# Weight preparation spread over an attention stage, and side work of the following MLP moved between items

## The chip, the core and the metric

The kernel runs on one core of a Trainium2 chip. Its engines are TensorE (PE in the rows; its weight loads are PEld), VectorE (DVE), ScalarE (ACT) and GpSimd (POOL); all loads and stores are issued on SyncE's queue (SP). Each engine works through its own queue in order. The metric is the device time in microseconds.

## What is computed

Three models in a row, on 2304 tokens of 512 features. Inputs are fp32; the products run on fp16 halves of scaled operands.

```python
# 1: causal attention with decay, 4 batches x 8 heads, S = 576, D = 64
scores = q @ k.T / 8 + decay;  attn = softmax(causal(scores));  x = attn @ v      # -> (2304, 512)
# 2: MLP with cosine
h = x @ w_in;  x = (h * cos(h)) @ w_out                                            # 512 -> 2048 -> 512
# 3: MoE, 8 experts, gate normalised over rows and columns eight times
P = sinkhorn(exp(x @ w_gate - max));  out = sum_e P[:, e] * (relu(x @ w1[e]) @ w2[e])   # 512 -> 1024 -> 512
```

## The kernel before

The program's order is written out by hand and nothing is rescheduled: each engine executes its instructions as the code issues them.

**Stages.** The attention takes 0 to about 240 us. It goes through 16 pairs of heads, seven steps `x` a pair, 112 steps, and a few more in which the pipeline drains. The MLP takes 240 to 645 us. Its 2048 hidden features are 16 units of 128, in blocks `b` of 3, 4, 5 and 4 units; its tokens are five chunks `j` of 384, 384, 512, 512 and 512. An item is one unit on one chunk, 80 items in the order block, chunk, unit. For each item `layer1` issues 12 products into a bank, `between` computes h cos(h) with three operations of ScalarE (L283, L286, L289) and three of VectorE (L285, L288, L291), and two items later (`LAG`) `layer2` issues 12 products into the output tile. When the last unit of a block is through, `finish` takes the sum out (L970, L972, L974). The MoE fills the rest.

**Weight units.** The MLP's weights arrive as 64-bit words in fp32 pairs and are put into fp16 halves a unit at a time. `read_unit` takes two half units of 128x512: for each a guard product `dm` on GpSimd (L175), four operations on VectorE (L176, L178, L180, L183, the last of which reads `dm`) and a square on ScalarE (L185). `scale_unit` finds the scale. `split_unit` scales each half on ScalarE (L202) and splits it on GpSimd (L164, L165). A `yield` ends each piece. In the attention one piece is issued in every second step from step 4, and in every step from 104; units 0 to 2 are through by step 86, unit 3 is read in steps 88 to 104 and scaled in 105 to 107. The rest follows between the items, from `work`.

**Other side work.** `split_row` splits the attention's output on GpSimd (L227, L164, L165); the last chunk's rows are split at items 1, 3, 5 and 7. The survey takes the absolute maximum of the MoE's weights: 64 looks of 128x1024 on ScalarE (L906), each on a 512 KB load (L902) into one of two buffers, one look in each of items 0 to 63. `find_scale` makes a scale of the results: of w1 after item 32, of w2 after item 64, of x0 (the MoE's input of chunks 0 and 1) from item 70. `split_x` prepares a chunk for the gate with four times ScalarE L991 and VectorE L992 and L993; for chunks 0 and 1 all four at once, where the block is finished, at items 64 and 68. `scale_first` (L1087) scales x0 at items 73 and 74; GpSimd's `combine_first` (L1308, L1309, L1312) builds the MoE's operands of it.

Of the kernel before, what the change touches and what calls it, by code (L numbers as in the profile page):

```python
# [23 lines left out]
def kernel(  # L24
# [39 lines left out]
    TOP = 14  # L64
    LIMIT = 36
# [30 lines left out]
    dm = big.tile([P, DM], BF16, name="dm")  # L96
    XT = [big.tile([P, 2, KD, n], F16, name=f"xt{j}") for j, (_, n) in enumerate(CH)]
    spare_bank = []
    sq = big.tile([P, NQ * P], BF16, name="sq")
# [66 lines left out]

    def read_unit(u):
        tm, ws = tmw[u % len(tmw)], wsum[u % 3]
        for half in range(2):
            n = 2 * u + half  # L170
            words = stg[n % 2].rearrange("p (c two) -> p c two", two=2)
            top, low, topf = words.bitcast(I32)[:, :, 1], words.bitcast(I32)[:, :, 0], words[:, :, 1]
# [10 lines left out]
            nc.vector.scalar_tensor_tensor(x, dm, TINY * TINY, x, ALU.is_ge, ALU.mult)  # L183
            yield
            nc.scalar.activation(sq[:, 0:DM], x, AF.Square, accum_out=ws[:, half : half + 1])  # L185
# [62 lines left out]

    turns = {}
# [24 lines left out]
    def between(b, j, i, ps):  # L274
        n = CH[j][1]
        u = unit(b, i)
# [17 lines left out]
    with tc.manual_schedule():  # L294

        with ExitStack() as actx:
# [22 lines left out]
            E4 = ap1.tile([P, SP], F32, name="e4")  # L319
            v_hi = [ap1.tile([P, NF, 2, D + 1], F16, name=f"vh{i}") for i in range(2)]  # L320
# [151 lines left out]
            def square_v(n):  # L472
                vr = raw[n][2]
                nc.scalar.activation(
                    sq.rearrange("p (t h d) -> p t h d", h=2, d=D), vr[:, :, :, 0:D], AF.Square,
# [312 lines left out]
            pieces = chain(chain.from_iterable(run_unit(u) for u in range(NWA)), read_unit(NWA), scale_unit(NWA))  # L788
# [41 lines left out]
            for x in range(-9, NSTEP + PS):  # L830
# [13 lines left out]
                if x >= 4 and (x % 2 == 0 or x >= NSTEP - 8):  # L844
                    next(pieces, None)
# [4 lines left out]
                if x == NSTEP - 2 * PS:  # L850
# [3 lines left out]
                if x == NSTEP - 3:  # L854
                    assert not list(scaling)
# [4 lines left out]
            for _ in pieces:  # L860
# [862 lines left out]
```

## Time and profile before

| | us |
|---|---|
| median of 3 runs (1983.05 to 1984.57) | 1984.53 |
| the profiled execution | 1984.58 |
| its span | 1982.9 |
| busy: TensorE / VectorE / ScalarE / GpSimd | 1925.6 / 1481.5 / 1207.2 / 1112.9 |

TensorE is busy for 97% of the span, the granted clock of the span is 0.998 of full speed. A row of busy time by stretch gives for each engine the busy microseconds in it, with the instructions in brackets, then the granted clock, the busy share of the DMA engines and what they moved. In a timeline a row stands for one or several equal instructions in a row, with start, duration, engine, line, operation and tiles; in square brackets is how long the engine had been idle before it, and what ended that.

### The profile page before, as it was taken

Reading aid. Unit: us, or ns where it says so; the run is one execution under the profiler, and the core shown is the slowest. Engines: PE = TensorE matmul, PEld = TensorE weight load, DVE = VectorE, ACT = ScalarE, POOL = GpSimd, SP = SyncE. Lnnn points to the kernel's source line nnn. Section 1 sums busy time; section 2 is a strip of 40 time slices with the busy share of each in tenths; the row PEclk is TensorE's granted clock in tenths of the full one; section 3 lists DMA queues with packets and bytes.
Section 4 is the critical chain, followed back from the end, with each engine's and each line's share of the span. In section 5 each row is a group of like instructions: output and inputs, shape, how many; then the busy total and the mean of one; then the engine's idle time right before and its main releaser. Section 6 shows DMA issues by size and latency. Waiting matters only on the chain.

```text
span 1982.9 us, 38801 instructions
## 1 busy us (share of the span) xinstructions
PE 1925.6 (97%) x14490; PEld 1371.4 (69%) x14490; DVE 1481.5 (75%) x3263; ACT 1207.2 (61%) x2439; POOL 1112.9 (56%) x1549
## 2 busy tenths in 40 slices
PE   6999989999999999999999999999999999999998
PEld 5788745454544677777777777777777777777776
DVE  8888788786566578887777777777777777777776
ACT  7999778777644765555565555555555555556543
POOL 6788875323067886454654555645556555565531
PEclk9999999999999999999999999999999999999999
DMA  5545355553302022202022021220212202122022
GB/s 127 113 97 119 76 172 180 156 172 118 117 22 78 19 81 89 75 25 88 33 78 78 23 89 33 78 78 22 89 33 78 78 22 88 33 78 78 12 88 65
DMA packets 133916, 157.51 MB, mean 79 GB/s; under 512 B 63840, under 2 KB 98016, under 8 KB 133728
## 3 DMA queue, kind: packets, MB, share of 16 engines
q1 hardware_dynamic: 133728, 155.03, 25.9%
q8 instruction: 114, 1.87, 0.4%
q14 instruction: 74, 0.61, 0.1%
HBM read 139.71 MB, written 10.37 MB: 76 GB/s over the span
## 4 chain that ended last, share of the span: by engine, by line
PE 81%; DVE 9%; ACT 6%; POOL 2%; issue 2%; DVEq 0%; ACTq 0%; POOLq 0%
PE y L1588 19%; PE y L1467 18%; PE bq L1588 14%; PE bq L1467 14%; PE a L956 7%; PE ph L264 6%; DVE A L680 1%; ACT E L648 1%; ACT A L672 1%; DVE ph L288 1%; PE pst L660 1%; ACT t L286 1%; DVE acc L974 1%; DVE xl L992 1%; DVE t L285 1%
## 5 line engine op out<-in xcount | busy, mean ns | idle before, releaser
L1588 PEld LDWEIGHTS <-h 128*128 128x128 f16 x6048 | 590.6, 98 | 77.0 <-POOL h L1502 1.2
L1467 PEld LDWEIGHTS <-wa 128*128 128x128 f16 x4032 | 394.4, 98 | 259.2 <-issue 5.0
L1467 PE MATMUL y<-xc,wa 128*128 128x384 f16 x2304 | 430.6, 327 | 1.8 <-ACT ct L1483 1.0
L1502 POOL TENSOR_TENSOR h<-rt,h 128x384 f16<-128x384 f32 x192 | 175.5, 914 | 452.9 <-ACT h L1501 446.3
L1588 PE MATMUL y<-wb,h 128*128 128x256 f16 x3456 | 408.9, 273 | 0.9 <-POOL h L1502 0.9
L1483 ACT ACTIVATE ct<-y 128x384 f32<-128x384 f32 x192 | 94.4, 492 | 422.8 <-PE y L1467 422.6
L1467 PE MATMUL bq<-xc,wa 128*128 128x384 f16 x1728 | 329.1, 327 | 0.2 <-ACT ct L1483 0.2
L1588 PE MATMUL bq<-wb,h 128*128 128x256 f16 x2592 | 306.7, 273 | 0.2 <-DVE h L1493 0.2
L1569 DVE SCALAR_TENSOR_TENSOR acc<-y,gate,acc 128x256 f32<-128x256 f32 x504 | 212.6, 478 | 48.9 <-PE y L1588 48.9
L956 PE MATMUL a<-H,w 128*128 128x512 f16 (+1 forms) x960 | 201.4, 359 | 8.1 <-ACT acc L970 3.1
L264 PE MATMUL ph<-xt,w 128*128 128x512 f16 (+1 forms) x960 | 199.8, 358 | 0.0
L1569 DVE SCALAR_TENSOR_TENSOR acc<-bq,gate,acc 128x256 f32<-128x256 f32 x378 | 159.7, 478 | 39.2 <-PE bq L1588 39.1
L956 PEld LDWEIGHTS <-w 128*128 128x128 f16 x960 | 93.3, 98 | 102.7 <-issue 12.6
L1493 DVE TENSOR_TENSOR h<-bq,h 128x384 f16<-128x384 f32 x288 | 158.1, 551 | 3.3 <-ACT h L1490 0.6
L1487 DVE SCALAR_TENSOR_TENSOR bq<-bq,ct 128x384 f32<-128x384 f32 x192 | 107.7, 561 | 64.9 <-PE bq L1467 64.0
L264 PEld LDWEIGHTS <-w 128*128 128x128 f16 x960 | 93.5, 99 | 89.6
L1487 DVE SCALAR_TENSOR_TENSOR bq<-y,ct 128x384 f32<-128x384 f32 x96 | 54.4, 566 | 123.5 <-PE y L1467 118.1
L1490 ACT CAST h<-bq 128x384 f16<-128x384 f32 x288 | 134.7, 484 | 14.2 <-DVE bq L1544 14.0
L1496 POOL TENSOR_TENSOR h<-st,h 128x384 f16<-128x384 f32 x96 | 87.9, 916 | 84.9 <-ACT h L1490 79.8
L1500 ACT ACTIVATE rt<-bq 128x384 f32<-128x384 f32 x192 | 93.7, 488 | 21.5 <-DVE bq L1487 18.8
L1248 POOL TENSOR_TENSOR tm<-sg 128x256 f32<-128x256 f32 x128 | 92.4, 733 | 15.1 <-POOL h L1496 12.3
L1501 ACT ACTIVATE h<-bq 128x384 f16<-128x384 f32 x192 | 94.3, 491 | 0.0
(269 smaller groups left out, 3219.6 us busy)
## 6 DMA issues: line engine op xcount, KB each, us to landing
xc<-xd SPq DMA_DIRECT2D x105, 384.0 KB
seen<-in_moe_w_dram SPq DMA_DIRECT2D x64, 512.0 KB
sg<-in_moe_w_dram SPq DMA_DIRECT2D x64, 512.0 KB
stg<-in_moe_w_in_dram SPq DMA_DIRECT2D x16, 512.0 KB
stg<-in_moe_w_out_dram SPq DMA_DIRECT2D x16, 512.0 KB
xd<-xc SPq DMA_DIRECT2D x14, 384.0 KB
q<-q SPq DMA_DIRECT2D x30, 160.0 KB
out_dram<-acc SPq DMA_DIRECT2D x18, 256.0 KB
```

The lines of the kernel that those rows point to most:

```text
L264: nc.tensor.matmul(ps[:, 0:n], w[:, ws, kk * P : (kk + 1) * P], XT[j][:, xs, kk, :], start=first, stop=kk == KD - 1 and (ws, xs) == PASSES ...
L956: nc.tensor.matmul(a_of[b, j][x][:, 0:n], w[:, s1, DM + x * P : DM + (x + 1) * P], H[:, s2, 0:n], start=i == 0 and n_ == 0, stop=end and n ...
L1467: nc.tensor.matmul(ps[:, 0:HN], w[:, ws, a, k, :], X[b][:, xs, k, :], start=fresh and n == 0, stop=n == 5, skip_group_check=not fresh,)
L1483: nc.scalar.activation(c, cut(ps), AF.Copy, scale=RAISE)
L1487: nc.vector.scalar_tensor_tensor(cut(c), cut(ps), RAISE, other, ALU.mult, ALU.add)
L1490: nc.scalar.copy(HT[m][c][:, 0, :], src)
L1493: nc.vector.tensor_tensor(HT[m][c][:, 1, :], src, HT[m][c][:, 0, :], ALU.subtract)
L1500: nc.scalar.activation(r, cut(ps), AF.Relu)
L1501: nc.scalar.activation(HT[m][c][:, 0, :], cut(ps), AF.Relu)
L1502: nc.gpsimd.tensor_tensor(HT[m][c][:, 1, :], r, HT[m][c][:, 0, :], ALU.subtract)
L1569: nc.vector.scalar_tensor_tensor(a, v, gate[:, tt, e : e + 1], a, ALU.mult, ALU.add)
L1588: nc.tensor.matmul(ps[:, at_ * HD : (at_ + 1) * HD], HT[m][a][:, s1, c * P : (c + 1) * P], W2T[side][m][:, s2, b, :], start=fresh and m == ...
```

## The change

1. In the attention the pieces of units 0 to 2 come at 46 in 102 steps, evenly, from step 6 to 97. Unit 3 is read in the drain, one piece a step from step 107; its scaling moves behind the first items. The factors that depend on units 0 to 2 are formed at step 109 instead of 98 and 109.
2. In the attention GpSimd scales the unit's halves, in place of ScalarE; between the items ScalarE still does (`late_`).
3. The guard product is issued half a unit ahead, into one of two buffers.
4. No look in items 0 to 7, one in items 8 to 35, two in each from 36 until they are done (item 53). The scale of w1 and w2 follow then: w2's small operations move from items 65 to 68 to items 55 to 58.
5. Chunks 0 and 1 of the gate are split two rows at a time, behind the next two items' own operations.
6. x0's scale is found from item 71, `scale_first` runs at items 74 and 75, and the last chunk's rows are split at items 2, 4, 6 and 8.

The number of instructions on TensorE and VectorE stays.

```diff
+    dms = [big.tile([P, DM], BF16, name=f"dm{i}") for i in range(2)]
...
+    def guard(n):
+        if n < len(jobs):
+            top = words_of(n)[2]
+            nc.gpsimd.tensor_tensor(dms[n % 2], top, top, ALU.mult)
...
     def read_unit(u):
...
-            nc.gpsimd.tensor_tensor(dm, topf, topf, ALU.mult)
+            if n == 0:
+                guard(0)
             nc.vector.tensor_scalar(xi, top, 3, 0x3FFFFFFF, ALU.logical_shift_left, ALU.bitwise_and)
             yield
             nc.vector.scalar_tensor_tensor(xi, top, -0x40000000, xi, ALU.bitwise_and, ALU.bitwise_or)
+            guard(n + 1)
             yield
...
-            nc.vector.scalar_tensor_tensor(x, dm, TINY * TINY, x, ALU.is_ge, ALU.mult)
+            nc.vector.scalar_tensor_tensor(x, dms[n % 2], TINY * TINY, x, ALU.is_ge, ALU.mult)
...
-            nc.scalar.activation(tm[:, c], tm[:, c], AF.Copy, scale=sc_w[:, u, half : half + 1])
+            if late_[0]:
+                nc.scalar.activation(tm[:, c], tm[:, c], AF.Copy, scale=sc_w[:, u, half : half + 1])
+            else:
+                nc.gpsimd.tensor_scalar(tm[:, c], tm[:, c], sc_w[:, u, half : half + 1], 0.0, ALU.mult, ALU.add)
...
+    SEEN_FIRST, SEEN_TWICE = 8, 36
...
         nc.scalar.activation(t.bitcast(I32), h, AF.Identity, bias=quarter, scale=sc)
-        next(looking[0], None)
+        if SEEN_FIRST <= now_:
+            next(looking[0], None)
         nc.vector.scalar_tensor_tensor(t, h, sc, t.bitcast(I32), ALU.mult, ALU.subtract)
         nc.scalar.activation(t, t, AF.Sin, scale=TWO_PI, bias=shift)
+        if now_ >= SEEN_TWICE:
+            next(looking[0], None)
         next(pieces, None)
...
-                if x >= 4 and (x % 2 == 0 or x >= NSTEP - 8):
-                    next(pieces, None)
+                if x >= 4:
+                    owed += 46 / (NSTEP - 10)
+                    if owed >= 1:
+                        owed -= 1
+                        next(pieces, None)
+                if x >= NSTEP - 5:
+                    for _ in pieces:
+                        pass
+                    next(fourth, None)
...
-                    if j < 2:
-                        next(splits)
-                    else:
-                        at(after_l2, step + x // 2, lambda: next(splits))
+                    at(after_l2, step + x // 2, lambda: next(splits))
...
-            flow = [chain(split_unit(NWA), done_unit(NWA))]
+            flow = [finish_unit(NWA)]
...
-        schedule_scale("x0", largest[:, 0 : 2 * KD], 70)
+        schedule_scale("x0", largest[:, 0 : 2 * KD], 71)
...
-            at(after_l2, 73 + x // 2, lambda x=x: scale_first(x))
+            at(after_l2, 74 + x // 2, lambda x=x: scale_first(x))
...
-            if n in (1, 3, 5, 7):
-                split_row(NCH - 1, n // 2)
+            if n in (2, 4, 6, 8):
+                split_row(NCH - 1, n // 2 - 1)
```

The diff also moves a scratch tile, writes late squares into the unit's own place in `W`, and changes a constant of the scales (`TOP` to `TOP_E`), which is a number only. In the rows of the changed kernel a line stands 1 to 29 further down.

VectorE at the end of the attention, before (A and xp are tiles of the attention, tmw a weight half, ph a bank of the MLP):

```order
L680 SCALAR_TENSOR_TENSOR A<-pst,A 128x512
L727 TENSOR_SCALAR rc_159<-pv,scv 128x4
L725 TENSOR_SCALAR rc_159<-pv 64x2
L728 RECIPROCAL rc_159<-rc_159 128x6
L730 TENSOR_TENSOR xp<-pv,rc_159 128x4x64
L730 TENSOR_TENSOR xp<-pv,rc_159 64x128
L285 SCALAR_TENSOR_TENSOR t_4404<-ph,turnv,t_4404 128x384
L288 SCALAR_TENSOR_TENSOR ph<-ph,lift,t_4404 128x384
L291 TENSOR_TENSOR H_4403<-ph,H_4403 128x384
L176 TENSOR_SCALAR tmw_4449<-stg_71 128x512
```

The same place after:

```order
L701 SCALAR_TENSOR_TENSOR A<-pst,A 128x512
L194 SCALAR_TENSOR_TENSOR tmw_73<-dm_77,tmw_73 128x512
L186 TENSOR_SCALAR tmw_73<-stg_72 128x512
L188 SCALAR_TENSOR_TENSOR tmw_73<-stg_72,tmw_73 128x512
L748 TENSOR_SCALAR rc_160<-pv,scv 128x4
L746 TENSOR_SCALAR rc_160<-pv 64x2
L749 RECIPROCAL rc_160<-rc_160 128x6
L751 TENSOR_TENSOR xp<-pv,rc_160 128x4x64
L751 TENSOR_TENSOR xp<-pv,rc_160 64x128
L191 SCALAR_TENSOR_TENSOR tmw_73<-stg_72,tmw_73 128x512
L303 SCALAR_TENSOR_TENSOR t_4398<-ph,turnv,t_4398 128x384
L308 SCALAR_TENSOR_TENSOR ph<-ph,lift,t_4398 128x384
```

Four pieces of unit 3 (L194, L186, L188, L191) now stand around the attention's last normalisation, in front of the first item's L303, which was L285.

ScalarE in items 36 and 37, before (seen is a look's buffer):

```order
L283 ACTIVATE t_6047<-ph,quarter,turnv 128x384
L906 ACTIVATE seen_4454,found_4464<-seen_4454 128x1024
L286 ACTIVATE t_6047<-t_6047,shift 128x384
L289 CAST H_6046<-ph 128x384
L283 ACTIVATE t_6089<-ph,quarter,turnv 128x384
L906 ACTIVATE seen_4453,found_4464<-seen_4453 128x1024
L286 ACTIVATE t_6089<-t_6089,shift 128x384
L185 ACTIVATE sq,wsum_84<-tmw_73 128x512
L289 CAST H_6088<-ph 128x384
```

And after:

```order
L300 ACTIVATE t_6025<-ph,quarter,turnv 128x384
L935 ACTIVATE seen_4449,found_4459<-seen_4449 128x1024
L304 ACTIVATE t_6025<-t_6025,shift 128x384
L935 ACTIVATE seen_4450,found_4459<-seen_4450 128x1024
L309 CAST H_6024<-ph 128x384
L300 ACTIVATE t_6069<-ph,quarter,turnv 128x384
L935 ACTIVATE seen_4449,found_4459<-seen_4449 128x1024
L304 ACTIVATE t_6069<-t_6069,shift 128x384
L935 ACTIVATE seen_4450,found_4459<-seen_4450 128x1024
L197 ACTIVATE w_4439,wsum_84<-tmw_73 128x512
L309 CAST H_6068<-ph 128x384
```

A second look stands between an item's second and third operation.

VectorE where chunk 0 leaves the MLP, before (acc is the output, xl the gate's operand):

```order
L974 SCALAR_TENSOR_TENSOR acc<-a_7093,down,acc 128x384
L992 TENSOR_TENSOR xl_4447<-acc,xl_4447 128x384
L993 TENSOR_REDUCE largest<-acc 128x1
L992 TENSOR_TENSOR xl_4447<-acc,xl_4447 128x384
L993 TENSOR_REDUCE largest<-acc 128x1
L992 TENSOR_TENSOR xl_4447<-acc,xl_4447 128x384
L993 TENSOR_REDUCE largest<-acc 128x1
L992 TENSOR_TENSOR xl_4447<-acc,xl_4447 128x384
L993 TENSOR_REDUCE largest<-acc 128x1
L285 SCALAR_TENSOR_TENSOR t_7226<-ph,turnv,t_7226 128x384
L288 SCALAR_TENSOR_TENSOR ph<-ph,lift,t_7226 128x384
L291 TENSOR_TENSOR H_7225<-ph,H_7225 128x384
```

And after:

```order
L1003 SCALAR_TENSOR_TENSOR acc<-a_7108,down,acc 128x384
L303 SCALAR_TENSOR_TENSOR t_7225<-ph,turnv,t_7225 128x384
L308 SCALAR_TENSOR_TENSOR ph<-ph,lift,t_7225 128x384
L311 TENSOR_TENSOR H_7224<-ph,H_7224 128x384
L1018 TENSOR_TENSOR xl_4443<-acc,xl_4443 128x384
L1019 TENSOR_REDUCE largest<-acc 128x1
L1018 TENSOR_TENSOR xl_4443<-acc,xl_4443 128x384
L1019 TENSOR_REDUCE largest<-acc 128x1
L303 SCALAR_TENSOR_TENSOR t_7268<-ph,turnv,t_7268 128x384
L308 SCALAR_TENSOR_TENSOR ph<-ph,lift,t_7268 128x384
L311 TENSOR_TENSOR H_7267<-ph,H_7267 128x384
L1018 TENSOR_TENSOR xl_4443<-acc,xl_4443 128x384
```

The item's own three operations come before the split, and half of the split goes to the item behind.

## Rows read from the trace of the kernel before

**Rows 1.** The page, chain of work that ended last: share of the span by engine.

```profile
PE 81%; DVE 9%; ACT 6%; POOL 2%; issue 2%; DVEq 0%; ACTq 0%; POOLq 0%
```

**Rows 2.** Busy time by stretch: the first items, the middle, the gate.

```profile
240.00:276.00 36.00, 31.09 (x183) 17.45 (x181) 27.57 (x48) 25.11 (x50) 25.81 (x31) 1.00 0.54 176
400.00:545.00 145.00, 145.00 (x765) 74.65 (x764) 97.22 (x163) 98.81 (x181) 32.48 (x51) 1.00 0.44 138
545.00:585.00 40.00, 35.73 (x189) 18.75 (x188) 27.13 (x52) 16.83 (x30) 30.42 (x42) 1.00 0.09 27
```

**Rows 3.** Busy time by stretch, head pairs: order PE, PEld, DVE, ACT, POOL.

```profile
87.46:102.31 14.85, 12.75 (x148) 11.12 (x147) 14.22 (x39) 12.58 (x28) 11.20 (x16) 1.00 0.58 119
115.90:128.94 13.04, 12.58 (x149) 11.27 (x149) 10.96 (x37) 12.75 (x26) 10.69 (x21) 1.00 0.44 98
212.10:226.31 14.21, 12.44 (x144) 10.76 (x143) 13.49 (x43) 12.38 (x26) 11.97 (x17) 1.00 0.23 62
226.31:239.03 12.72, 11.30 (x136) 9.40 (x135) 7.94 (x27) 7.80 (x16) 11.05 (x25) 1.00 0.01 2
```

**Rows 4.** ScalarE's weight scalings: group by line, 20 to 236 us; chain of waits.

```profile
L202 ACT ACTIVATE tmw<-tmw,scw 128x512 f32<-128x512 f32 x6 | 4.3, 716 | 0.0
```

```profile
129.55 0.61 ACT tmw L202
```

**Rows 5.** GpSimd by line, 20 to 236 us: busy us, mean ns | idle before.

```profile
L464 POOL TENSOR_SCALAR vrest<-vraw,scv 128x512 f32<-128x512 f32 x15 | 12.1, 810 | 1.0
```

**Rows 6.** Timeline around 95 us, GpSimd and VectorE.

```profile
94.73 1.42 POOL L513 TENSOR_TENSOR k<-ktf,k 64x576 fp32r<-64x576 f32 x1
94.90 1.80 DVE L183 SCALAR_TENSOR_TENSOR tmw<-dm,tmw 128x512 f32<-128x512 bf16 x1
```

**Rows 7.** Timeline 256 to 264 us.

```profile
257.28 1.04 POOL L175 TENSOR_TENSOR dm<-stg 128x512 bf16<-128x512 f32 x1
...
258.35 0.69 DVE L183 SCALAR_TENSOR_TENSOR tmw<-dm,tmw 128x512 f32<-128x512 bf16 x1 [2.58 <-POOL dm L175]
...
260.62 1.05 ACT L970 ACTIVATE acc<-a,down 128x384 f32<-128x384 f32 x2
261.24 0.65 PE L956 MATMUL a<-H,w 128*128 128x384 f16 x3 [2.74 <-ACT acc L970]
```

**Rows 8.** Timeline of TensorE and ScalarE in the MLP; busy time during one look's load.

```profile
286.60 2.75 PE L956 MATMUL a<-H,w 128*128 128x512 f16 x12
289.19 2.75 PE L264 MATMUL ph<-xt,w 128*128 128x512 f16 x12
```

```profile
406.98 0.67 ACT L283 ACTIVATE t<-ph,quarter,turnv 128x384 int32<-128x384 f32 x1 [0.70 <-PE ph L264]
407.55 1.04 ACT L906 ACTIVATE seen<-seen 128x1024 f32<-128x1024 f32 x1
```

```profile
502.25:504.30 2.05, 2.05 (x11) 0.97 (x10) 1.15 (x2) 0.59 (x1) 0.00 (x0) 1.00 0.79 254
```

**Rows 9.** Timeline 550 to 553 us; TensorE's waits, 545 to 590 us (total, times, longest).

```profile
550.98 0.54 DVE L993 TENSOR_REDUCE largest<-acc 128x1 f32<-128x384 f32 x1
...
553.02 0.61 ACT L286 ACTIVATE t<-t,shift 128x384 f32<-128x384 f32 x1 [3.68 <-DVE t L285]
```

```profile
PE a L956 <- ACT H L289: 2.1, 2, 1.6
PE pl L1006 <- DVE H L291: 1.5, 1, 1.5
```

**Rows 10.** Waits of GpSimd, 590 to 690 us, and of TensorE, 590 to 680 us.

```profile
POOL xc L1308 <- ACT acc L1087: 21.6, 2, 16.8
POOL h L1502 <- ACT h L1501: 6.7, 2, 4.8
POOL xs L1344 <- ACT acc L1332: 1.7, 1, 1.7
```

```profile
PE y L1588 <- POOL h L1502: 0.9, 1, 0.9
```

More of the change, by code (lines that the diff above doesn't have):

```diff
@@ L64 @@
     TOP = 14
+    TOP_E = 12
     LIMIT = 36
@@ L95 @@
         W[s] = big.tile([P, 2, 2 * DM], F16, name=f"w{s}")
-    dm = big.tile([P, DM], BF16, name="dm")
+    dms = [big.tile([P, DM], BF16, name=f"dm{i}") for i in range(2)]
     XT = [big.tile([P, 2, KD, n], F16, name=f"xt{j}") for j, (_, n) in enumerate(CH)]
     spare_bank = []
-    sq = big.tile([P, NQ * P], BF16, name="sq")
+    junk = []
     wsum = [big.tile([P, 2], F32, name=f"wsum{i}") for i in range(3)]
@@ L165, in halves, with words_of @@
         nc.gpsimd.tensor_tensor(lo, src, hi, ALU.subtract)
+    def words_of(n):
+        words = stg[n % 2].rearrange("p (c two) -> p c two", two=2)
+        return words.bitcast(I32)[:, :, 1], words.bitcast(I32)[:, :, 0], words[:, :, 1]
+    def guard(n):
+        if n < len(jobs):
+            top = words_of(n)[2]
+            nc.gpsimd.tensor_tensor(dms[n % 2], top, top, ALU.mult)
     def read_unit(u):
@@ L170, in read_unit @@
             n = 2 * u + half
-            words = stg[n % 2].rearrange("p (c two) -> p c two", two=2)
-            top, low, topf = words.bitcast(I32)[:, :, 1], words.bitcast(I32)[:, :, 0], words[:, :, 1]
+            top, low, _ = words_of(n)
             x = tm[:, half * DM : (half + 1) * DM]
             xi = x.bitcast(I32)
-            nc.gpsimd.tensor_tensor(dm, topf, topf, ALU.mult)
+            if n == 0:
+                guard(0)
             nc.vector.tensor_scalar(xi, top, 3, 0x3FFFFFFF, ALU.logical_shift_left, ALU.bitwise_and)
@@ L275, in between @@
         n = CH[j][1]
+        now_ = items.index((b, j, i))
         u = unit(b, i)
@@ L319 @@
             E4 = ap1.tile([P, SP], F32, name="e4")
+            junk.append(ap1.tile([P, NQ * P], BF16, name="sq"))
             v_hi = [ap1.tile([P, NF, 2, D + 1], F16, name=f"vh{i}") for i in range(2)]
@@ L787 @@
                 put(n, "x_act", keep_x, n)
-            pieces = chain(chain.from_iterable(run_unit(u) for u in range(NWA)), read_unit(NWA), scale_unit(NWA))
+            pieces = chain.from_iterable(run_unit(u) for u in range(NWA))
+            fourth = read_unit(NWA)
+            owed = 0.0
             scaling = iter(())
@@ L849 @@
                     split_row(*rows.pop(0)[1:])
-                if x == NSTEP - 2 * PS:
+                if x == NSTEP - 3:
+                    assert not list(scaling) and not list(pieces)
                     block_factors(0)
@@ L853 @@
                         turn_factors(u, 0, 3)
-                if x == NSTEP - 3:
-                    assert not list(scaling)
                     for u in range(NWA):
@@ L859 @@
             quiet[0] = True
-            for _ in pieces:
+            for _ in fourth:
                 pass
@@ L925, in find_scale @@
             nc.vector.tensor_scalar(
-                scale.bitcast(I32), back.bitcast(I32), -1.0, float((254 + TOP) << 23), ALU.mult, ALU.add
+                scale.bitcast(I32), back.bitcast(I32), -1.0, float((254 + TOP_E) << 23), ALU.mult, ALU.add
             )
-            nc.vector.tensor_scalar(back, back, 2.0**-TOP, None, ALU.mult)
+            nc.vector.tensor_scalar(back, back, 2.0**-TOP_E, None, ALU.mult)
             yield
@@ L1073 @@
         looking[0] = survey()
-        PER = 1
-        schedule_scale("w1", found[0], NSEEN // PER + 1)
-        schedule_scale("w2", found[1], 2 * NSEEN // PER + 1, 3)
+        looks = [(n, z) for n in range(len(items)) for z in range((n >= SEEN_FIRST) + (n >= SEEN_TWICE))]
+        schedule_scale("w1", found[0], looks[NSEEN][0] + 1)
+        schedule_scale("w2", found[1], looks[2 * NSEEN][0] + 1, 3)
         assert items[69 - LAG] == (NB1 - 1, 1, tiles_of(NB1 - 1) - 1) and sum(m for _, m in CH[:2]) == 768
-        schedule_scale("x0", largest[:, 0 : 2 * KD], 70)
+        schedule_scale("x0", largest[:, 0 : 2 * KD], 71)
         assert items[77 - LAG] == (NB1 - 1, 3, tiles_of(NB1 - 1) - 1)
```

5 lines of the change are left out of this document (3 added, 2 removed).

## The prediction

> **What bounds the kernel now.** I read the chain of waits first, then busy time by stage, then each stage's own waits. The chain is TensorE for 81% of the span [rows 1], so only what makes TensorE idle or late counts. By stage [rows 2]: from 400 to 545 us TensorE is busy 145.00 of 145 us and nothing can be won there; from 240 to 276 us it lacks 4.9 us of 36; from 545 to 585 us it lacks 4.3 of 40. The change touches all of these, the attention before them and the start of the MoE behind them. In the attention the length of a head pair is the measure: 13.04 us at best, 14.85 us where most weight pieces fall, with ScalarE busy 12.6 to 12.8 us of either [rows 3]. So ScalarE is nearly full in the attention, and VectorE nearly so in the longest pair (14.22 of 14.85).
>
> The sum is made against the profiled execution's 1984.58 us (span 1982.9 and 1.7 around it); the median of the runs shown is 1984.53, so the two are the same for this purpose. What the measurement can tell from no change is about 0.2%, 4.0 us: "faster" means below 1980.6.
>
> **Attention, body: about -2.3 us.** The pieces of weight units 0 to 2 keep their number and are only spread differently (28 steps a unit before, about 31 after). Their own cost is read from the four pairs of unit 1, 55.54 us together, of which the longest and the shortest are shown [rows 3], against four times 13.04, so 3.4 us a unit; spreading moves it and I book nothing. Unit 3's reading leaves the body: the pair in which most of it runs takes 14.21 us, 1.2 above the best [rows 3], so -1.2. The six scalings leave ScalarE: 4.3 us in all [rows 4], of which the chain holds three, at 0.61 us each like the one shown [rows 4]. So the gain lies between 0 (the other half of a unit's chain is late anyway) and 4.3; I take the chain's 1.8. GpSimd gets them: the nearest row is its own scaling of a tile of 128x512, 810 ns [rows 5], so 4.9 us more on an engine that has 2 to 3 us free in each pair (10.69 to 11.97 busy [rows 3]). That costs 0 if the free time takes it, 4.9 if the key tiles behind it, which GpSimd prepares for TensorE, are always awaited; I take 0.7, one scaling in six, since the chain holds 2% of GpSimd in all [rows 1]. The guard products half a unit earlier cost nothing: no VectorE piece in the body waits for one now, and the two buffers take the wait that GpSimd would have for the old one.
>
> What decides how long a weight piece takes is what GpSimd does then. VectorE's L183 takes 1.80 us at 94.90, while GpSimd's L513 runs from 94.73 to 96.15, and 0.69 where nothing meets it, at 258.35 [rows 6, 7]. The Trainium skill ("SBUF — State Buffer", section "SBUF: two separate sides") says that VectorE and GpSimd share a pair of ports as an exclusive lock: an operation with two SBUF inputs waits for the whole of a GpSimd operation, while ScalarE has its own port. The row agrees (1.80 is close to what was left of L513 and 0.69 behind it), and by that rule the move of the scalings from ScalarE to GpSimd could cost the whole 4.9 us, which would make the sum below -1.0 instead of -5.2.
>
> **Attention, drain: +0.8 us.** Eight VectorE pieces and two squares of unit 3 now lie in the last steps and beside the first items. From 226.31 to 239.03 VectorE is busy 7.94 of 12.72 us [rows 3], so most fit into holes. One L180 stands ahead of the first item's L285 (see the order), at 0.7 to 1.1 us; the ends are +0.5 and +1.5. The factors of the lifts, moved to the last steps, are small operations of GpSimd and VectorE (0.2 to 0.3 us each, an estimate from the drain's timeline) and are hidden by the last row splits.
>
> **Transition 240 to 276 us: -2.5 us.** TensorE's longest stop there is 2.74 us at 261.24. Backwards: the first scaling of the block's output (L970, 260.62) stands on ScalarE behind work that waits for VectorE, and VectorE waits 2.58 us in L183 for the guard product that GpSimd only does at 257.28, behind row splits and halves [rows 7]. After the change that product is half a unit ahead, the row splits start one item later, and ScalarE has no looks of 1.05 + 0.19 us in items 0 to 7. So this wait goes. What is next late: VectorE has three weight pieces an item there, and unit 3's two scalings (0.7 us each) now stand on ScalarE ahead of that same L970. By the rows' durations TensorE resumes some 1.7 us earlier than now, and of the other 2.2 us of small stops I give back 0.8, for the looks. Ends: 0 and -4.5 (nearly all of the 4.9).
>
> **Middle, items 8 to 53: +1.0 us.** One look an item hides now, as TensorE's 145 of 145 shows. From item 36 there are two. Items 36 to 44 have 384 columns: TensorE's products of 512 columns come 2.59 us apart, 5.18 an item [rows 8], so 3.9 for three quarters of it. ScalarE needs 0.57 for L283 (from its start to the next), 1.04 for the look [rows 8], 0.61 for L286 [rows 9], a second look of 1.04 to 1.24 and a cast of about 0.4, so 3.8 us, and the nine items hold nine more squares and scalings at about 0.65 (near the 716 ns of the scaling in [rows 4]): 40 us against TensorE's 35.1. ScalarE falls behind by 4.6 to 5 us. An item's second product comes two items behind its first, 7.8 us, and its chain takes about 4.5 with two looks (an estimate: those 3.7 and VectorE's last operation of 0.6): about 3.3 us of slack, so some 1.5 is left, of which the looser items around them return a part. The 512-column items behind give slack again. The loads: one look's 512 KB takes 2.05 us at 254 GB/s and a share of 0.79 [rows 8]; two an item need 4.1 of 3.9 us where they don't overlap, and up to a quarter less where they do. Ends: 0 and +6.
>
> **Gate, 545 to 585 us: -3.7 us.** At 546 VectorE does four L974 (2.2 us) and then four pairs of L992 and L993 (1.1 us a pair, 0.54 of it L993) in front of the next item's L285; ScalarE's L286 waits 3.68 us and TensorE stands still; it happens again at 579 for chunk 1 (2.1 us of TensorE's waits at both), and at 561.6 TensorE waits 1.5 us for a bank and VectorE [rows 9]. Those 4.3 us are the stage's whole lack. With two pairs behind an item's own chain, 2.2 us a step, VectorE has 1.8 + 2.2 = 4.0 us of work in an item of 3.9 to 5.2 us, so the stall goes but for the four L974. The second weight scale's small products move to items 55 to 58, where TensorE has work ahead. Ends: -2.0 and -4.3.
>
> **Into the MoE, 585 to 660 us: +1.5 us.** x0's scale is found one item later, and GpSimd's first combination waits for exactly that: 16.8 us at its longest [rows 10]. One item is 5.2 us. From there GpSimd works almost without a gap into the MoE, where it has 1.7 us of waiting for L1332 and 1.9 for L1501 to give; the 4.8 us wait in the same row comes after the start. So 5.2 - 3.7 = 1.5, on top of a TensorE stall of 0.9 behind GpSimd that is there now [rows 10]. Ends: 0 (TensorE has other work) and +5.2.
>
> **Sum:** -2.3 + 0.8 - 2.5 + 1.0 - 3.7 + 1.5 = -5.2, so 1979.4 us.
>
> **Rivals.**
> *More of it* (1973.8): attention -3.0 with the drain, transition -4.0, gate -4.3, middle 0, MoE +0.5, in all -10.8. For it: each of these stops has a named cause that the change removes. Against: VectorE is as full in the first items as before.
> *Two looks bind* (1984.6): the middle costs the full 6 instead of 1.0, by loads that come late to the second look and a ScalarE that never catches up; -0.2. For it: the 40 against 35.1; against: the slack of two items and the share of 0.44 over that stretch [rows 2].
> *GpSimd late into the MoE* (1983.1): the whole item, 5.2 instead of 1.5; -1.5. For it: the 0.9 us stall is there now. Against: 3.7 us of waits before it.
> *Slower: GpSimd against VectorE in the attention* (1989.3). Weight pieces now come at every phase of a pair, and GpSimd has six operations more. Each meeting of the kind at 94.90 costs 1.1 us (1.80 - 0.69) on a chain that has no slack in the long pair; nine more of them among 24 VectorE pieces cost 9.9, and -5.2 becomes +4.7. Below nine it is no longer slower. This is the shared lock of the Trainium skill's page "SBUF — State Buffer", section "SBUF: two separate sides". For it: six operations more on GpSimd and no slack on ScalarE's side of a pair. Against: of the ten L183 up to 262 us three take 1.77 to 1.80 us now, the one shown and two like it, so that an even spread would meet GpSimd about as often.
> *That it does nothing:* the orders show that the operations move as the words say, so this has no case of its own.
>
> **How the numbers follow.** Forecast 0.42 (1976.5 to 1983), more of it 0.17, two looks 0.13, late GpSimd 0.12, slower 0.16. Of the forecast's 0.42 some 0.33 lies under 1980.6, so faster is 0.33 + 0.17 = 0.50; within 0.2% is 0.09 + 0.13 + 0.12 = 0.34; slower 0.16. The range 1973.5 to 1989.0 leaves out half of the best rival and half of the slower one, 0.16.
>
> **What would show it.** Right: no stop of over 1 us before TensorE's L956 around 260 or 550 us, at least 3 us more TensorE share in those two stretches; head pairs with scalings under 13.8 us; GpSimd's wait for the first scaling longer, and its start in the MoE tighter. Wrong: pairs of 14.5 us and more with L183 at 1.8 us many times; waits for the look's load, or TensorE under 100% between items 36 and 44; a stop of 3 us or more at the first MoE products behind GpSimd.

## The result, and the profile after

The changed kernel takes 2001.55 us (median of 6 runs, 2000.77 to 2003.17) against 1984.44 us of the kernel before beside it: 1.0087 times as long, with a 95% interval of 1.0074 to 1.0100. The forecast was 1979.4 us, and its range ended at 1989.0. The profiled execution has a span of 2001.4 us, 18.5 us more.

To see where, each product of TensorE is matched with the same product of the kernel before, by line and number, and the difference of their starts is taken. The column on the left says when the product starts in the kernel before.

```
at, us   place                                    after is behind by
  239    the attention's last pv                   +1.2
  247    third item's first product                +6.0
  264    sixth item                                +2.0
  284    tenth item                                +3.1
  358    block 1, second chunk                     +4.4
  426    before the two looks                      +3.9
  442    in the two looks, 384 columns            +14.4
  460    first item of 512 columns                +16.8
  523    two looks done                           +19.7
  547    gate, chunk 0 leaves the MLP             +19.7
  593    behind the gate's splits                 +13.7
  645    first product of the MoE                 +13.8
  721    MoE under way                            +18.2
 1957    end                                      +18.4
```

Three places lose most: the first items (1.9 us from 239 to 284, and 1.3 more by 358), the two looks (15.8 from 426 to 523) and the start of the MoE (4.4); one gains, the gate (6.0). The chain of waits of the page, in answer to [rows 1]:

```profile
PE 70%; DVE 6%; ACT 4%; POOL 3%; DMA 2%; issue 2%; SPq 0%; DVEq 0%; POOLq 0%
```

TensorE has 70% of it in place of 81%, and DMA, which had no share, has 2%: the survey's loads. Busy time by stretch of the kernel after, as in [rows 2], with the middle cut in two:

```profile
240.00:276.00 36.00, 32.18 (x199) 18.75 (x198) 30.12 (x50) 18.69 (x37) 29.48 (x35) 0.95 0.32 100
400.00:450.00 50.00, 43.23 (x243) 23.55 (x241) 33.51 (x61) 35.75 (x69) 9.25 (x13) 1.00 0.61 193
450.00:500.00 50.00, 46.90 (x227) 22.66 (x227) 30.55 (x52) 40.01 (x77) 15.58 (x27) 0.97 0.68 214
545.00:585.00 40.00, 39.99 (x233) 23.24 (x232) 25.34 (x43) 17.69 (x33) 28.16 (x40) 1.00 0.08 27
```

TensorE, which was never idle from 400 to 545 us, now lacks 6.8 of 50 us and then 3.1 of 50. ScalarE is not full in either, 35.75 and 40.01 of 50: it waits too. The stretch from 545 to 585 us, which lacked 4.3 us, lacks nothing; since the changed kernel is 19.7 us late at the gate, its own gate lies from 565 on, and from 565 to 605 us TensorE is busy 39.99 of 40 us, too. One stop of 1.7 us stands behind it, at 612 us, before the gate's product of chunk 1. The granted clock is below 1 in two stretches.

**The two looks.** ScalarE in the nine items of 384 columns (timeline; idle time before and its end in brackets), and two issues on SyncE's queue:

```profile
430.80 1.06 ACT L935 ACTIVATE seen<-seen 128x1024 f32<-128x1024 f32 x1 [1.11 <-DMA seen<-in_moe_w_dram]
...
433.64 1.06 ACT L935 ACTIVATE seen<-seen 128x1024 f32<-128x1024 f32 x1 [0.75 <-DMA seen<-in_moe_w_dram]
...
436.54 1.06 ACT L935 ACTIVATE seen<-seen 128x1024 f32<-128x1024 f32 x1 [1.24 <-DMA seen<-in_moe_w_dram]
```

```profile
431.98 0.33 SPq L931 DMA_DIRECT2D seen<-in_moe_w_dram  x1
432.41 0.38 SPq L124 DMA_DIRECT2D stg<-in_moe_w_in_dram  x1
```

The look at 430.80 frees its buffer at 431.86; the next load into it is issued at 431.98, a weight load follows at 432.41, and the look at 436.54 finds it just landed, 4.56 us after the issue. A buffer's round is therefore a look and a load in a row, 1.2 + 4.5 us, and two buffers give two looks in 5.7 us, in an item for which TensorE needs 3.9. Waits from 425 to 545 us (in total, times, longest):

```profile
ACT seen L935 <- DMA seen<-in_moe_w_dram: 16.6, 20, 1.6
...
PE ph L280 <- DVE H L311: 3.9, 2, 2.5
...
PE pl L947 <- DVE gm L944: 3.2, 1, 3.2
```

TensorE is not named with the loads. It stops for what is behind them: a bank that an item's last VectorE operation frees late, and L947, a small product for w1's scale. L947 does not wait for a look of w1, the last of which ended at 426.12: it waits for L944, which stands on VectorE behind an item's L311, and that L311 waits 2.08 us for a cast that ScalarE does only behind the look at 436.54.

**The first items.** VectorE and ScalarE, then TensorE (timeline):

```profile
239.72 0.97 DVE L194 SCALAR_TENSOR_TENSOR tmw<-dm,tmw 128x512 f32<-128x512 bf16 x1
240.62 0.83 DVE L186 TENSOR_SCALAR tmw<-stg 128x512 int32<-128x512 int32 x1
241.49 1.52 DVE L188 SCALAR_TENSOR_TENSOR tmw<-stg,tmw 128x512 int32<-128x512 int32 x1
...
248.31 0.63 ACT L197 ACTIVATE sq<-tmw 128x512 bf16<-128x512 f32 x1 [1.28 <-DVE tmw L194]
248.85 0.19 ACT L197 ACTIVATION_READ_ACCUMULATOR sq<-tmw 128x1 f32 x1
248.94 0.62 ACT L765 COPY acc<-psx 128x576 f32<-128x576 f32 x1
...
249.61 3.03 PE L985 MATMUL a<-H,w 128*128 128x384 f16 x12 [2.95 <-ACT acc L765]
```

The three pieces of unit 3 take 3.3 us, the attention's last normalisation comes behind them, and unit 3's second square waits for VectorE while L765, which TensorE needs, stands behind it. The wait and the square hold L765 back from 247.03 to 248.94, which is 1.9 of TensorE's 2.95 us.

**The start of the MoE**, in answer to [rows 10]: TensorE's and GpSimd's waits.

```profile
PE y L1614 <- POOL h L1528: 3.9, 1, 3.9
```

```profile
POOL xc L1334 <- ACT acc L1113: 44.1, 2, 39.1
```

GpSimd waits 22 us longer for x0 than before, mostly because the whole MLP ends 13.8 us later. What it had to give before the first products, 1.7 us of waiting for L1332 and 1.9 for L1501 [rows 10], is used up; the wait of 4.8 us behind them is still there. TensorE waits 3.9 us instead of 0.9.

### The profile page after: what moved, and what is told of

Its sections match the earlier page's. It is cut to its first block, busy times and chain, and to the rows that moved or that the text cites. A ratio compares the mean times of both kernels' runs of the same rounds, so it can differ in the third digit from the quotient of the medians.

```text
span 2001.4 us, 38797 instructions
## 1 busy us (share of the span) xinstructions
PE 1932.4 (97%) x14490; PEld 1373.7 (69%) x14490; DVE 1486.5 (74%) x3263; ACT 1204.6 (60%) x2433; POOL 1117.6 (56%) x1555
## 4 chain that ended last, share of the span: by engine, by line
PE 70%; DVE 6%; ACT 4%; POOL 3%; DMA 2%; issue 2%; SPq 0%; DVEq 0%; POOLq 0%
PE y L1614 19%; PE y L1493 18%; PE bq L1614 14%; PE bq L1493 13%; PE a L985 3%; PE ph L280 3%; DMA seen<-in_moe_w_dram 2%; ACT t L304 1%; DVE ph L308 1%; DVE t L303 1%; ACT seen L935 1%; DVE acc L1003 1%; ACT H L309 1%; POOL xc L1335 1%; DVE tmw L191 0%
## 5 line engine op out<-in xcount | busy, mean ns | idle before, releaser
L1528 POOL TENSOR_TENSOR h<-rt,h 128x384 f16<-128x384 f32 x192 | 175.3, 913 | 451.1 <-ACT h L1527 444.1
L304 ACT ACTIVATE t<-t,shift 128x512 f32<-128x512 f32 (+1 forms) x80 | 54.0, 675 | 74.3 <-DVE t L303 74.2
```

What stands on the lines that cost most here:

```text
L1528: nc.gpsimd.tensor_tensor(HT[m][c][:, 1, :], r, HT[m][c][:, 0, :], ALU.subtract)
```

## Experiments

Times are medians; each is given with its ratio to the kernel before in the same comparison. "Behind" and "ahead" are differences of starts as in the table above, from the profiled executions.

### The survey

**The survey alone on the kernel before.**

```diff
+        if now_ >= 8:
+            next(looking[0], None)
...
+        if now_ >= 36:
+            next(looking[0], None)
```

> The kernel before with the survey's new places alone: no look in items 0 to 7, one in items 8 to 35, two from item 36. Theory: the same loss as in the changed kernel, about 14 to 16 us in items 36 to 54, less 2 us or so in the first items, which have no looks: 1996 to 2001 us. Rival (the loss needs the other edits beside it, the later scaling of unit 3 or the guard products): under 1991 us.

1997.99 us, 1.0074 (1.0059 to 1.0089): the theory, though the two looks lose 13.3 us here and not 14 to 16. Behind by 1.3 us at 426, 9.0 at 442 and 14.6 at 523; the clock is at half for 6.8 us from 437, which is some 3.4 of it. The absence of looks in the first items gave 1.7 us at 252 and lost it by 264, where the clock was at half for 6.8 us.

**The looks without their loads.**

```diff
-                load_chunk(n + 2)
+                if n + 2 < 28:
+                    load_chunk(n + 2)
```

> The changed kernel without the survey's loads from the 29th look on: ScalarE looks at the same buffers again, as often and in the same places, so part of the maximum over the MoE's weights is left out. Theory A (the second look waits for its load: the trace shows 16.6 us of such waits in ScalarE, 20 times): the loss of 15.8 us shrinks to 4 us or less, 1986 to 1991 us. Theory B (ScalarE is too full with two looks, 40 us of work against 35 us of TensorE's in nine items; the loads only come late because it is late): it stays above 1996 us.

1990.76 us, 1.0040 (1.0026 to 1.0055): theory A, whose 4 us are just missed. From 426 to 523 us the loss is 4.2 us (3.6 to 7.8), not 15.8, with the same looks in the same places:

```profile
400.00:450.00 50.00, 48.34 (x278) 27.08 (x276) 39.00 (x72) 40.01 (x80) 11.69 (x16) 1.00 0.22 71
450.00:500.00 50.00, 49.15 (x240) 23.20 (x238) 33.51 (x56) 44.94 (x86) 17.25 (x31) 1.00 0.10 33
```

ScalarE does more in each stretch than in the kernel after, and TensorE lacks 1.7 and 0.9 us. So ScalarE's work costs some 4 us, and the loads with what hangs on them the other 11.6; L947's stop and the half clock at 452 us are gone with them. These loads also shared the queues with the weights', which is in that figure. Whether a third buffer would have been enough was not tried: from 430 to 445 us the changed kernel's DMA share is 0.81 already, at 256 GB/s.

**One look an item, the rest of the change kept.**

```diff
-    SEEN_FIRST, SEEN_TWICE = 8, 36
+    SEEN_FIRST, SEEN_TWICE = 0, 999
```

> The changed kernel with the survey as it was: one look in each of items 0 to 63, the scales of w1 and w2 found behind items 32 and 64; everything else changed. Between items 36 and 54 the changed kernel falls behind the kernel before by 15.8 us (from +3.9 us at TensorE's product of 422 us to +19.7 at 523 us). Theory (two looks in an item cause that loss, nothing else does): those 15.8 us go, and some 1 to 3 us come back as looks in the first items and as w2's small products beside the gate, so 1986 to 1989 us. Rival (the loss there comes from the weight units, whose scaling and guard products were moved too): it stays above 1995 us.

1995.19 us, 1.0060 (1.0043 to 1.0077): the rival's time, but not its place. The middle lost nothing any more (7.6 us behind at 358, at 426 and at 547), so the two looks were its cause; but by 358 the first blocks lost 3 us more with their looks in them, and the gate gave nothing (7.6 behind at 547, 7.8 at 593). The edits hang together: the gap in the survey paid for a part of the late unit 3, and the early end of the survey paid for the gate.

### x0

```diff
-                    at(after_l2, step + x // 2, lambda: next(splits))
+                    at(after_l2, step + (x // 2 if j != 1 else 0), lambda: next(splits))
...
-        schedule_scale("x0", largest[:, 0 : 2 * KD], 71)
+        schedule_scale("x0", largest[:, 0 : 2 * KD], 70)
...
-            at(after_l2, 74 + x // 2, lambda x=x: scale_first(x))
+            at(after_l2, 73 + x // 2, lambda x=x: scale_first(x))
```

> The changed kernel with x0's scale an item earlier, at item 70 as before, and scale_first at items 73 and 74; for that chunk 1 is split at one go behind item 69's own operations. Theory (GpSimd comes an item later into the MoE, which costs the stop of 3.9 us before TensorE's y at 677.8 us and the half clock that follows it): 3.5 to 5.5 us faster than the changed kernel, 1996 to 1998 us. Rival (GpSimd is late there for another reason, the preparation of weights in front): within 1 us of it, 2000.5 to 2002.5 us.

1996.92 us, 1.0069 (1.0054 to 1.0084): the theory. It is 4.6 us less than the changed kernel by the medians, and 3.5 when each is taken against the kernel before beside it (13.6 us and 17.1 above). It is 12.4 us behind both at 645 and at 690, where the changed kernel goes from 13.8 to 18.2, and TensorE's wait for L1528 is 0.9 us again.

### The attention and unit 3

**The attention's pieces alone on the kernel before** (spread, and unit 3 in the drain).

```diff
-                if x >= 4 and (x % 2 == 0 or x >= NSTEP - 8):
-                    next(pieces, None)
+                if x >= 4:
+                    owed += 46 / (NSTEP - 10)
...
+                if x >= NSTEP - 5:
+                    for _ in pieces:
+                        pass
+                    next(fourth, None)
...
-            flow = [chain(split_unit(NWA), done_unit(NWA))]
+            flow = [finish_unit(NWA)]
```

> The kernel before with the attention's pieces alone as in the change: 46 in 102 steps, unit 3 read in the drain, its scaling behind the first items; guard products, scalings on ScalarE and everything else as before. The prediction gave -1.2 us in the body and +0.8 us in the drain. Theory now (the reading in the drain puts VectorE's pieces and ScalarE's squares in front of the first items, and unit 3's scaling in front of the next): 5 to 10 us behind the kernel before by item 20, 1989 to 1994 us. Rival (the delay needs the guard products, which GpSimd does in the drain ahead of the row splits): under 3 us behind by item 20, 1983 to 1987 us.

1985.64 us, 1.0013 (1.0004 to 1.0022): the rival. The drain does cost, from +0.2 us at 239 to +5.5 at 247, but by 264 all but 1.2 of it is regained, and 2.5 stay at 284.

**Unit 3 early, on the kernel with one look.** It takes the attention's order of pieces of the kernel before, and keeps GpSimd's scalings and the guard products ahead.

```diff
-                if x >= NSTEP - 5:
-                    for _ in pieces:
-                        pass
-                    next(fourth, None)
+                if x >= 4 and (x % 2 == 0 or x >= NSTEP - 8):
+                    next(pieces, None)
...
-            flow = [finish_unit(NWA)]
+            flow = [chain(split_unit(NWA), done_unit(NWA))]
```

> The changed kernel with one look an item as before, and with the attention's pieces as before: a piece every second step, unit 3 read in steps 88 to 104 and its scale found there; GpSimd still scales units 0 to 2 and the guard products are still half a unit ahead. With one look an item alone the kernel was at 1995.2 us, 7.6 us behind the kernel before at item 20 to item 64, of which 1.1 us are lost in the attention, 3.6 at the first item and the rest until item 22. Theory (reading and scaling unit 3 late is what costs there): the 7.6 us shrink to 2 or less, 1988 to 1990 us. Rival (GpSimd's scalings and guard products do it): 4 us or more of delay stay by item 22, 1992 us or more.

1986.46 us, 1.0021 (1.0012 to 1.0031), 8.7 us less than with the late unit: the theory, and by more than was expected. It is 1.7 us ahead of the kernel before at 239 and 4.6 ahead at 264, where the late unit left 1.1 and 3.8 behind. Two things are undone in this edit, the late unit and the spreading: 2.8 us of the difference are there at 239, at the attention's end, and 5.5 more come from 239 to 264. What it still loses is x0's item (4.6 us from 645 to 721) and the gate's stop.

**Even pieces with unit 3 inside the attention**, on the kernel called "guard ahead" below.

```diff
-                if x >= 4 and (x % 2 == 0 or x >= NSTEP - 8):
-                    next(pieces, None)
+                if x >= 4:
+                    owed[0] += 58 / 104
```

> The run with the guard products ahead, and the same pieces of units 0 to 3 spread evenly over the attention's steps, 58 in 104, with unit 3 still read inside the attention. Theory (only unit 3's late reading costs; even spreading does not): the attention's end stays 1.5 to 2 us ahead of the kernel before. Rival (pieces at every phase of a pair meet GpSimd more often: the changed kernel was 1.2 us behind at the attention's end though unit 3 was no longer in it): 0 to 3 us behind at that place, and the whole 2 to 4 us slower than the run with the old order.

1982.26 us, 0.9991 (0.9982 to 1.0000): the rival's time, 4.3 us slower than with the old order by the medians and 3.8 when each is taken against the kernel before beside it. At 239 us it is 2.4 us behind, where the old order is 1.8 ahead, so spreading costs 4.2 in this kernel. The rival's mechanism shows little of it. VectorE's weight pieces from 20 to 236 us, first with the old order, then spread evenly (by line: busy us, mean ns):

```profile
L194 DVE SCALAR_TENSOR_TENSOR tmw<-dm,tmw 128x512 f32<-128x512 bf16 x8 | 8.9, 1110 | 0.0
L191 DVE SCALAR_TENSOR_TENSOR tmw<-stg,tmw 128x512 int32<-128x512 int32 x8 | 7.2, 894 | 0.0
L188 DVE SCALAR_TENSOR_TENSOR tmw<-stg,tmw 128x512 int32<-128x512 int32 x8 | 7.0, 876 | 0.0
L186 DVE TENSOR_SCALAR tmw<-stg 128x512 int32<-128x512 int32 x8 | 4.3, 533 | 0.0
```

```profile
L194 DVE SCALAR_TENSOR_TENSOR tmw<-dm,tmw 128x512 f32<-128x512 bf16 x8 | 8.1, 1009 | 0.0
L188 DVE SCALAR_TENSOR_TENSOR tmw<-stg,tmw 128x512 int32<-128x512 int32 x8 | 7.6, 953 | 0.0
L191 DVE SCALAR_TENSOR_TENSOR tmw<-stg,tmw 128x512 int32<-128x512 int32 x8 | 6.9, 866 | 0.0
L186 DVE TENSOR_SCALAR tmw<-stg 128x512 int32<-128x512 int32 x8 | 5.7, 709 | 0.0
```

Together 27.4 us and 28.3: VectorE needs 0.9 us more for the pieces, so the rest of the harm comes from where they fall. Of the evenly spread kernel's waits of TensorE in that stretch, 2.3 us are for GpSimd's k (L534), against 1.3 in the old order, and 2.4 us for ScalarE's E (L669), which the longest waits of the old order don't show:

```profile
PE pv L731 <- ACT k L520: 2.7, 2, 1.5
PE pv L731 <- ACT E L669: 2.4, 4, 1.1
PE pss L625 <- POOL k L534: 2.3, 4, 1.1
```

The old order put a unit's 28 steps on exactly four pairs of seven, so each piece had its phase in the hand-made order of the pair. Why the other phases are worse, piece by piece, wasn't settled.

**The scalings back on ScalarE**, on the same kernel.

```diff
-            if late_[0]:
+            if True:
                 nc.scalar.activation(tm[:, c], tm[:, c], AF.Copy, scale=sc_w[:, u, half : half + 1])
```

> The run with the guard products ahead (two looks from item 45, stepwise gate, the attention's order of pieces as before, GpSimd's scalings) with the six scalings of the attention back on ScalarE. That run was 1.8 us ahead of the kernel before at the attention's end and 4.7 us ahead at 264 us. Theory (the scalings' move to GpSimd is worth the 1.8 us, the guard products the 2.9 us behind it): at 239 us within 0.5 us of the kernel before, at 264 us 2.5 to 3.2 us ahead, 1.5 to 2 us slower than that run in all. Rival (the guard products alone give both): level with it at both places.

1982.06 us, 0.9986 (0.9977 to 0.9995), some 4 us slower: with this order of pieces the scalings on GpSimd gain, by more than was expected. At 199 us the kernel is 0.2 us ahead of the one before, with GpSimd's scalings 3.6, so 3.4 us for six. (At 239 it is 2.8 behind, with a stretch of half clock at 219 in it, and at 264 level.) From 239 to 264 both gain 2.9 us, so that gain belongs to what they share, the guard products ahead and the later row splits, which no run parts.

With the pieces spread, as in the change itself, that gain isn't there. The pieces alone, with ScalarE's scalings and the old guard products, are 1.0 us behind at 199 and 0.2 at 239; the changed kernel, with GpSimd's scalings and the guard products ahead, is 2.8 and 1.2 behind. And there VectorE's pieces do get longer. Two of the four groups from 20 to 236 us, first of the pieces alone, then of the changed kernel:

```profile
L178 DVE SCALAR_TENSOR_TENSOR tmw<-stg,tmw 128x512 int32<-128x512 int32 x7 | 6.9, 982 | 0.0
L180 DVE SCALAR_TENSOR_TENSOR tmw<-stg,tmw 128x512 int32<-128x512 int32 x7 | 6.1, 875 | 0.0
```

```profile
L188 DVE SCALAR_TENSOR_TENSOR tmw<-stg,tmw 128x512 int32<-128x512 int32 x7 | 8.0, 1144 | 0.0
L191 DVE SCALAR_TENSOR_TENSOR tmw<-stg,tmw 128x512 int32<-128x512 int32 x6 | 6.5, 1083 | 0.0
```

The 24 pieces of units 0 to 2 take 23.2 us in the changed kernel and 19.9 with the pieces alone; in the old order it is 20.0 with GpSimd's scalings and 21.3 with ScalarE's. So what the scalings are worth depends on the order of the pieces. In the spread order no run parts them from the guard products.

### The gate

**The gate's split alone on the kernel before.**

```diff
-                    if j < 2:
-                        next(splits)
-                    else:
-                        at(after_l2, step + x // 2, lambda: next(splits))
+                    at(after_l2, step + (x // 2 if j != 1 else 0), lambda: next(splits))
```

> The kernel before with the gate's split alone: chunk 0 two rows at a time behind two items' own operations, chunk 1 at one go but behind item 69's own operations, so that x0's scale stays where it was. Theory of the prediction (the four pairs in front of an item's L285 cost TensorE the stops of 1.9 and 0.8 us, and more): 2 to 4 us faster, 1980 to 1982 us. Rival (the stage is held by VectorE's whole work there, with w2's small operations at items 65 to 68 in it: with one look an item and the stepwise split the changed kernel gained nothing between 546 and 630 us): within 1 us of the kernel before.

1985.43 us, 1.0012 (1.0002 to 1.0021): no gain, and 1.7 us slower, a little more than the rival's 1. TensorE's waits from 543 to 605 us:

```profile
PE pl L1003 <- DVE H L291: 3.9, 1, 3.9
```

The two stops for L289 in [rows 9] are gone, and the third one there, 1.5 us before the gate's product, has become 3.9: w2's small product and the gate's both take a bank of the ring that the items use. The clock is at half for 6.8 us behind this stop, some 3.4 us of time.

**With w2's scale out of the way**, by two looks from item 45, where the chunks have 512 columns.

```diff
+        if now_ >= 45:
+            next(looking[0], None)
```

> As the run before it, and the survey with one look in items 0 to 44 and two from item 45, where all chunks have 512 columns, so that w2's scale is found from item 55. Theory (two looks cost because items of 384 columns, 3.9 us, are shorter than two loads; 512 columns, 5.2 us, hold them; and the gate gains once w2's operations are out of its way): 4 to 6 us faster than before, 1977.5 to 1980 us. Rival (two looks cost there too, 2.5 us or more): 1981 us or more.

1979.40 us, 0.9983 (0.9974 to 0.9992): the theory, at the end of its bracket. The two looks cost 0.5 us there (+0.5 at 502, +1.0 at 523), and the gate's region goes from 1.0 behind at 547 to 4.6 ahead at 593, a gain of 5.6. The survey alone on the kernel before has w2's scale out of the way as well, without the split in steps: it gains 1.0 us between these places, with 3.4 us of half clock in them. So neither alone gives the 5.6; without the half clock, an estimate from half of each stretch, the split would gain 1.6 and w2's place 2.7.

### What remains of the change

**Guard ahead**: to this, the guard products half a unit ahead, GpSimd's scalings and the later row splits; not the spreading, not the late unit 3, not the later x0.

```diff
+            if n == 0:
+                guard(0)
...
+            guard(n + 1)
...
```

> As the run before it, and the guard products half a unit ahead, GpSimd's scalings in the attention, and the last chunk's rows split at items 2, 4, 6 and 8; the attention's order of pieces is the one of the kernel before. Theory of the prediction (the stop of 2.74 us at 261.24 goes, which waits for a guard product): 1.5 to 3 us faster than the run before it. Rival (VectorE is full in the first items and the stop only moves): within 1 us of it.

1977.96 us, 0.9969 (0.9958 to 0.9981). The median is 1.4 us under that of the run before, just short of the theory's 1.5; at 264 us this one is 4.7 us ahead of the kernel before, at 358 only 2.0. TensorE's longest wait between is 1.3 us, for the four operations of block 1's first sum, which follow a weight piece on VectorE. The two looks take 2.0 more.

**And no look in items 0 to 3**, two from 45 to 56.

```diff
-    SEEN_FIRST, SEEN_TWICE = 0, 45
+    SEEN_FIRST, SEEN_TWICE = 4, 45
```

> The run with the guard products ahead, with no look in items 0 to 3, so that the two looks an item run from item 45 to 56. Theory (the looks of the first items hold ScalarE where the block's first sums wait for it): 0.5 to 2 us ahead of that run at 284 us, and as much in all unless the two more items with two looks take it back. Rival (VectorE holds those items): level within 0.5 us at 284 us.

1975.90 us, 0.9956 (0.9944 to 0.9969), the best of all: 0.5 us further ahead at 284 (5.2 against 4.7) and 1.6 at 358, which is kept behind the two looks (at 547). It beats both kernels, the one before by 8.4 us.

One thing must be known to compare profiles here: TensorE's stop of 2.64 us at 740 us for the gate's normalisation, and the half clock behind it, are absent in the profiled executions of the gate's split alone, of the run after it and of guard ahead, which lie 4 to 5 us under their medians. Places are therefore compared before 721 us.

## Why the prediction was wrong, by its own steps

**Middle, +1.0, measured +15.8 from 426 to 523: the step that failed.** The prediction counted ScalarE's work (40 us against 35) and the moving time of a load (2.05 us), and set both against the time of an item. It did not put them in a row. A buffer's next load is issued when its look is over, and takes 4.56 us beside other loads, not 2.05; the round of two buffers is 5.7 us. The slack of two items was then used up by the third item with two looks, TensorE's first long stop (3.2 us) came one item later, and the slack was not returned while the two looks lasted. The 4.2 us that remain without loads are near the 4.6 to 5 by which the prediction had ScalarE fall behind, so the slack of 3.3 that it took off was not there either. The rival of the two looks named the mechanism, by loads that come late to the second look, with a chance of 0.13, but its price of 6 was the same count, and so less than half (its -0.2 makes 1984.4, not the 1984.6 beside it).

**Drain, +0.8, measured +4.8 (239 to 247).** Of the four pieces around the last normalisation one was priced, at 0.7 to 1.1 us, and the others were put into VectorE's idle time. They took 0.97, 0.83, 1.52 and 0.67, the first three more than the 0.68, 0.43 and 0.68 of the same lines at 247.53, 249.07 and 427.69, while GpSimd split rows and did a guard product. The two squares on ScalarE were named and given no price: one of them waits 1.28 us for VectorE with L765 behind it. Some 1.2 of the 4.8 us are the half clock behind that stop. Part of it came back by 264.

**Attention, -2.3, measured +1.2 at 239.** "Spreading moves it and I book nothing" failed: 4.2 us in the kernel with the guard products ahead. The scalings' gain is there in the old order only, where it is more than was booked (3.4 us against 1.8, less 0.7 on GpSimd); in the order of the change the scalings and the guard products together cost 1.0 to 1.8. By the port lock, which the Trainium skill ("SBUF — State Buffer", section "SBUF: two separate sides") states and the prediction weighed against this move, GpSimd's scalings should have cost VectorE time. In the old order the 24 pieces took 21.3 us with ScalarE's scalings and 20.0 with GpSimd's, which is no such cost; in the spread order they took 19.9 and 23.2, which is as the lock would have it, but the guard products were moved there too.

**Transition, -2.5.** Right where it stands alone: 2.9 us with unit 3 early. In the changed kernel the drain's loss came first; the 2.74 us stop is 1.2 us there.

**Gate, -3.7, measured -6.0.** Right in place, but put down to the wrong part. The rows it named hold 2.1 + 1.5 = 3.6 of the 4.3 us. The split in steps alone gains nothing, w2's early scale alone 1.0 us, both together 5.6. The prediction named that bank's 1.5 us and did not ask what it becomes when the stops ahead of it go.

**Start of the MoE, +1.5, measured +4.4.** The rival of a late GpSimd had the mechanism, and a price of 5.2. The 3.7 us of waits (the rows give 1.7 + 1.9 = 3.6) were to absorb most of it: with the late x0 they are used up, TensorE's own wait still rises by 3.0, and half clock follows.

**Slower, 0.16.** The side was in the list. The named mechanism, longer weight pieces on VectorE, is there (3.3 us over 24 pieces, where it wanted 9.9), but most of the time was lost elsewhere, in the two looks.

## What to carry to other kernels

The stream of loads through two buffers ran at the round of one buffer here, use and load in a row, and a load's time beside others was the one to count; set that round against the shortest item it must fit, and put the doubled rate where items are longest. When work is moved into a drain or a start, write down what stands behind each moved instruction on its queue, the waiting squares as well as the busy pieces. Edits that each look like a gain should be tried apart, and in the order that they will stand in: GpSimd's scalings gained with one order of pieces and not with the other. Here the part that was kept, with the doubled looks moved, was worth 8.4 us, and the whole cost 17.

## What the runs showed of the hardware

Three stops of TensorE of 2.5 to 3.9 us in the changed kernel were followed by a stretch at the lower of its two clock levels. Busy time by stretch, the stop and what follows, at the first items, in the two looks and at the MoE:

```profile
247.20:250.60 3.40, 0.99 (x7) 0.60 (x7) 1.88 (x4) 1.82 (x4) 0.85 (x2) 1.00 0.30 69
250.70:254.00 3.30, 3.30 (x14) 1.82 (x12) 3.30 (x6) 1.67 (x3) 3.22 (x4) 0.50 0.74 289
448.40:452.00 3.60, 1.23 (x8) 0.77 (x8) 2.81 (x4) 3.04 (x6) 1.98 (x3) 1.00 0.75 216
452.10:455.40 3.30, 3.30 (x12) 1.62 (x11) 2.76 (x9) 2.25 (x7) 0.30 (x1) 0.50 0.69 218
673.90:677.30 3.40, 0.00 (x0) 0.00 (x0) 1.28 (x3) 1.12 (x3) 3.40 (x5) 1.00 0.00 0
677.40:680.70 3.30, 2.91 (x14) 2.09 (x15) 0.00 (x0) 1.79 (x6) 3.30 (x5) 0.50 0.00 0
```

TensorE runs 3.3 us at a granted clock of 0.50 (1.2 instead of 2.4 GHz) and does half the work in it, so each of these stops costs about 1.7 us more than its own length. Not every such stop is followed by one: the 2.74 us before 261 us in the kernel before [rows 7] were not, nor the 3.2 us before L947 at 440 us in the changed one, while the same stop in the run with x0 early, 2.7 us long, was (0.50 from 440.2 to 443.4). Between the kernel's start and its last microseconds the changed kernel has five such stretches (the other two at 612 and 759 us) and the kernel before two (612 and 742); the three more are some 5 of its 18 us, which no term of the prediction held.
